# Two decode attentions on one core: the output layouts of step 31 moved ahead of A's wo matmuls, and the result's transposition in bf16

## The chip, the cores and the metric

The kernel runs on one core of a Trainium2 chip. The metric is the time of one execution on the device in microseconds. The kernel before took 675.33 us, the median of 3 runs from 673.68 to 675.58 us.

A core has five engines with a queue of instructions each: PE (TensorE, matrix products), DVE (VectorE), ACT (ScalarE), POOL (GpSimd) and SP (SyncE, which here issues the transfers). An engine works through its own queue in order and waits for others by semaphores.

## What is computed

Two attention blocks, A and B, decode one token each, with the same sizes: 32 heads of 128 elements, a cache of 8192 positions per head, a model width of 512. Everything is bf16. For each block:

```python
q = (x @ wq).reshape(B, Sq, H, Dh).transpose(0, 2, 1, 3)   # B = Sq = 1, H = 32, Dh = 128
scores = einsum("bhqd,bhkd->bhqk", q, k_cache) * Dh ** -0.5
p = softmax(scores, axis=-1)
o = einsum("bhqk,bhkd->bhqd", p, v_cache)
y = o.transpose(0, 2, 1, 3).reshape(B, Sq, H * Dh) @ wo     # wo is 4096 x 512
```

The output is y of A and y of B side by side, 1024 numbers. The caches of the two blocks are 256 MB and each byte of them is used once.

## The kernel before

**Steps.** A step handles one pair of heads: n = 0 to 15 are A's pairs, 16 to 31 are B's. Each pair has 4 MB of keys and 4 MB of values. A tile kn or vn holds one pair: the first head's positions lie on partitions 0 to 63, the second's on 64 to 127, 128 positions on each partition. There are two buffers of each.

**The scores.** DVE multiplies kn in place by the query, in four instructions of 32 positions each (`plan_mul`, L292). PE sums over the 128 elements of a head in two halves of 16 matmuls with the identity, accumulating in PSUM down to 8 columns per position (`plan_red`, L301), and DVE reduces the 8 (`plan_sr`, L310). These 32 matmuls of a step are called a batch here. Then come the maximum (`plan_max` L316 on DVE, `plan_gmax` L322 on PE and L325 on DVE, `plan_exp` L335 on PE and L339 on ACT), the exponentials on ACT (L346) and their sum (`plan_sum`: L351 on PE, the reciprocal L354 on DVE).

**The values.** `plan_pv` (L367) runs 128 matmuls with vn as weights and two columns of probabilities each. They belong to the pair before the one whose scores are being worked on, and lie between that step's score instructions. `plan_o` (L377) scales the result into oD, which holds for each head the 128 outputs on 128 partitions.

**The output product.** wo arrives in SBUF with 32 rows of wo on each partition for A, and for B in five groups of heads (0 to 15, 16 to 23, 24 to 27, 28 and 29, 30 and 31), which `WOG` lists. A group of h heads has h rows on each partition. The columns of oD have to be laid out to match: `plan_relayout` multiplies them with a mask into zb on DVE (L402), sums with a selection matrix on PE (L406, into the PSUM tile misc) and copies the result to o2 on DVE (L408). zb has two buffers and misc has one, so each matmul L406 waits for the copy L408 before it. `plan_wo` (L419) then multiplies wo with o2: four matmuls of one column for each head, all accumulating in the PSUM tile qyp; 128 in all for A. `plan_y` (L426) copies qyp to yT, 128 partitions by 4 columns for each block. At the end `plan_out` transposes yT with one matrix product against an identity (L430), DVE rounds the result to bf16 (L433), and SP writes 2 KB out.

**The order of the work.** There is no planner: a loop over n from 0 to 32 appends instructions to the queues of the five engines, and the order of the calls is the order in each queue. Ahead of an instruction stand the waits for what it needs. Between steps 3 and 30, PE's queue is emitted as a loop over two steps; step 31 and what follows is straight code. All large transfers are issued by SP. In step n these are the keys of step n + 1 and the values of step n, each waiting until its buffer is free. In step 31 SP issues the last values in two halves and then the five groups of B's wo, which go to the buffer of A's wo and so wait for A's last wo matmul (`load_wo`: `wo_done[0]`).

**Around the change.** At the start of step 31 (`L1` is 31) the kernel brings in the output product of A and B's first three groups, whose pairs are done by then. Later in step 31, behind the first two multiplications, DVE copies A's result (`plan_y(0)`). B's fourth and fifth group are laid out at the ends of steps 31 and 32, and B's 128 wo matmuls come last.

```python
if n == L1:
    plan_relayout(0, 0)
    plan_wo(0, 0)
    for g in range(3):
        plan_relayout(1, g)
```

Of the kernel before, what the change touches and what calls it, by code (L numbers as in the profile page):

```python
# [8 lines left out]
BF16 = mybir.dt.bfloat16  # L9
F32 = mybir.dt.float32  # L10

P = 128
# [11 lines left out]
class _Plan:  # L24
# [6 lines left out]
    def wait(self, eng, mark):  # L31
        if mark is None:
            return
        ctr, val = mark
        if val <= 0 or self.waited.get((eng, ctr.name), 0) >= val:
            return
        self.waited[(eng, ctr.name)] = val
        self.prog[eng].append((None, ctr, val))

    def op(self, eng, fn, ctr=None, needs=(), inc=1):  # L40

        for m in needs:
            self.wait(eng, m)
        self.prog[eng].append((fn, ctr, inc))
        if ctr is None:
            return None
        ctr.n += inc
        return ctr, ctr.n
# [46 lines left out]
def bass_concat_heads__mha_block_cached__gqa_block_cached__decode_kernel(  # L95
# [18 lines left out]
    NA = 2  # L114
# [22 lines left out]
    with ExitStack() as st:  # L137
# [3 lines left out]
        def sb(name, shape, dt):  # L141
            return ec(nc.sbuf_tensor(name, shape, dt))
# [14 lines left out]
        ident = sb("ident", [P, P], BF16)  # L157
        ident_f = sb("ident_f", [P, P], F32)
# [9 lines left out]
        mask = {g: sb("mask%d" % g, [P, P // g], BF16) for g in RG}  # L168
        jsel = {g: sb("jsel%d" % g, [P, g], BF16) for g in RG}
        NQ = NOUT // P  # L170
        yT = sb("yT", [P, NA, NQ], F32)
        out_q = sb("out_q", [NA * NQ, P], BF16)

        def ps(name, shape):
# [25 lines left out]
        def dma(eng, dst, src, c, needs=()):  # L200
            return op(eng, lambda e: e.dma_start(dst, src), c, needs, inc=16)  # L201
# [24 lines left out]
        def load_k(n):  # L226
            a, i = divmod(n, PA)
            src = ks[a][0, 2 * i:2 * i + 2].rearrange("h (p t) d -> (h p) (t d)", p=HP)
            k_in[n] = dma("SP", kn[:, n % NK].rearrange("p t d -> p (t d)"), src, s_k[n % NK],
                          [red_done.get(n - NK)])  # L230

        def load_v(n, parts=1):
            a, i = divmod(n, PA)
            src = vs[a][0, 2 * i:2 * i + 2].rearrange("h (p t) d -> (h p) (t d)", p=HP)
            dst = vn[:, n % NV].rearrange("p t d -> p (t d)")
            w = T * Dh // parts
            v_in[n] = [dma("SP", dst[:, i * w:(i + 1) * w], src[:, i * w:(i + 1) * w],
                           s_v2 if i else s_v[n % NV],
                           [q_done[1] if n == 1 else pv_done.get(n - NV)])
                       for i in range(parts)]  # L240
# [4 lines left out]
        def load_wo(a, g):  # L245
            h0, n = WOG[a][g]
            src = wos[a][h0 * Dh:(h0 + n) * Dh, :].rearrange("(p j) n -> p (j n)", p=P)
            wo_in[a, g] = dma("SP", wo_sb[:, h0:h0 + n, :].rearrange("p j n -> p (j n)"), src, s_wo[g],
                              [q_done[0] if a == 0 else wo_done[0]])
# [16 lines left out]
        def plan_q(a, j):  # L266

            def mm(e):
                r = None
                for hh in range(2):  # L270
                    for c in range(C):
                        w = wq_sb[a][:, c, 8 * j * Dh:8 * (j + 1) * Dh].rearrange(
                            "p (i h d) -> p i h d", h=2, d=Dh)[:, :, hh, :]
                        r = e.matmul(  # L274
                            qyp[hh * HP:(hh + 1) * HP, :].rearrange("p (i d) -> p i d", d=Dh),
                            xb[:, a, c, hh * HP:(hh + 1) * HP], w,
                            start=(c == 0), stop=(c == C - 1))
                return r
            m = op("PE", mm, c_pe, [x_ready, wq_in[a], qy_free[0]])
            q_done[a] = m  # L280
            n0 = a * PA + 4 * j
            qy_free[0] = op("ACT", lambda e: e.copy(
                qbc[:, n0:n0 + 4, :].rearrange("p i d -> p (i d)"), qyp[:]), c_act, [m])
            for n in range(n0, n0 + 4):
                qbc_ready[n] = qy_free[0]
# [4 lines left out]
        def plan_mul(n, c):  # L290
            k = kn[:, n % NK, c * CT:(c + 1) * CT, :]
            mul_done[n, c] = op("DVE", lambda e: e.tensor_tensor(  # L292
                k, k, qbc[:, n:n + 1, :].broadcast_to([P, CT, Dh]), ALU.mult),
                c_mul, [k_in[n], qbc_ready[n]])
# [101 lines left out]
        def plan_relayout(a, g):  # L396
            h0, n = WOG[a][g]
            z = z_n[0] % 2
            z_n[0] += 1
            s = P // n  # L400
            zv = zb[:, z, :].rearrange("p (h s) -> p h s", s=s)
            m = op("DVE", lambda e: e.tensor_tensor(  # L402
                zv, oD[:, a, h0:h0 + n].unsqueeze(2).broadcast_to([P, n, s]),
                mask[n][:, None, :].broadcast_to([P, n, s]), ALU.mult),
                c_dve, [sel_ready[n], o_done[a * PA + (h0 + n) // 2 - 1], z_free.get(z)])
            z_free[z] = op("PE", lambda e: e.matmul(misc[:, 0:n], zb[:, z, :], jsel[n][:],  # L406
                                                    start=True, stop=True), c_pe, [m, misc_free[0]])
            o2_ready[a, g] = misc_free[0] = op("DVE", lambda e: e.tensor_copy(  # L408
                o2[:, a, h0:h0 + n], misc[:, 0:n]), c_dve, [z_free[z]])

        def plan_wo(a, g):

            h0, n = WOG[a][g]

            def mm(e):
                r = None
                for j in range(h0, h0 + n):
                    for i in range(NQ):
                        r = e.matmul(qyp[:, i:i + 1], wo_sb[:, j, i * P:(i + 1) * P],  # L419
                                     o2[:, a, j:j + 1], start=(j == 0 and i == 0),  # L420
                                     stop=(j == H - 1 and i == NQ - 1), skip_group_check=True)
                return r
            wo_done[a] = op("PE", mm, c_pe, [o2_ready[a, g], wo_in[a, g], qy_free[0]])

        def plan_y(a):
            qy_free[0] = op("DVE", lambda e: e.tensor_copy(yT[:, a, :], qyp[:, 0:NQ]), c_dve,  # L426
                            [wo_done[a]])

        def plan_out():
            m = op("PE", lambda e: e.matmul(bmp[0:NA * NQ, 0:P], yT[:].rearrange("p a q -> p (a q)"),  # L430
                                            ident_f[:], start=True, stop=True),
                   c_pe, [qy_free[0], nb_done[NP - 1]])
            m = op("DVE", lambda e: e.tensor_copy(out_q[:], bmp[0:NA * NQ, 0:P]), c_dve, [m])  # L433
            done = dma("SP", out[0].rearrange("o (q n) -> (o q) n", q=NA * NQ), out_q[:], s_out, [m])
            wait("SP", done)
# [11 lines left out]
        for n in range(NP + 1):  # L447
            marks[n] = len(pl.prog["PE"])
            last = n == NP
            if n == L1:  # L450
                plan_relayout(0, 0)
                plan_wo(0, 0)
                for g in range(3):
                    plan_relayout(1, g)
            if n + 1 < NP:
                load_k(n + 1)
            if n == 1:
                for j in range(4):
                    plan_q(1, j)
            if not last:  # L460
                load_v(n, 2 if n == NP - 1 else 1)
            if n == 12:
                load_wo(0, 0)
            if n == NP - 1:
                for g in range(len(WOG[1])):
                    load_wo(1, g)
            if not last:
                plan_mul(n, 0)
                plan_mul(n, 1)
            if n == L1:  # L470
                plan_y(0)
            if n > 0:
                plan_sum(n - 1)
            if not last:
                plan_red(n, 0)
                plan_mul(n, 2)
                plan_mul(n, 3)
                plan_sr(n, 0)
                plan_red(n, 1)
            if n > 0:  # L480
                plan_pv(n - 1, 0, HT)
            if not last:
                plan_sr(n, 1)
                plan_max(n)
                plan_gmax(n)
            if n > 0:
                plan_pv(n - 1, HT, T)
            if not last:
                plan_exp(n)
            if n > 0:  # L490
                plan_o(n - 1)
            if n >= L1:
                plan_relayout(1, n - L1 + 3)
        for g in range(len(WOG[1])):
            plan_wo(1, g)
        plan_y(1)
        plan_out()

        for name, at in (("SP", block.sync), ("PE", block.tensor), ("ACT", block.scalar),
# [38 lines left out]
```

## Time and profile before

| | before |
|---|---|
| median of the runs | 675.33 us (673.68 to 675.58) |
| the profiled execution | 675.39 us |
| its span, first to last instruction | 673.7 us |
| mean granted clock of PE | 0.744 |
| PE busy | 469.2 us (70%) |
| DVE busy | 359.5 us (53%) |
| ACT busy | 43.9 us (7%) |
| read from HBM | 285.21 MB, 423 GB/s over the span |

All times inside the execution are microseconds from the start of the span. The profile's page gives the busy time of the engines, the span in 40 slices with the granted clock and the share in which the transfer engines were busy, the chain of work that ended last, and groups of equal instructions. The trace behind it gives the same chain in order of time, the timeline of each engine, and for each transfer the time from issue to landing. In a timeline a row has its start, its duration, the engine and line, the output and the input with their shapes, and how many instructions are merged in it; square brackets hold the idle time of the engine just before it and what ended that.

Matmuls of PE are pipelined: a row of 128 matmuls with 164 ns each lasts 3.6 us, not 21.

### The profile page before, as it was taken

Reading aid. Unit: us, or ns where it says so; the run is one execution under the profiler, and the core shown is the slowest. Engines: PE = TensorE matmul, PEld = TensorE weight load, DVE = VectorE, ACT = ScalarE, POOL = GpSimd, SP = SyncE. Lnnn points to the kernel's source line nnn. Section 1 sums busy time; section 2 is a strip of 40 time slices with the busy share of each in tenths; the row PEclk is TensorE's granted clock in tenths of the full one; section 3 lists DMA queues with packets and bytes.
Section 4 is the critical chain, followed back from the end, with each engine's and each line's share of the span. In section 5 each row is a group of like instructions: output and inputs, shape, how many; then the busy total and the mean of one; then the engine's idle time right before and its main releaser. Section 6 shows DMA issues by size and latency. Waiting matters only on the chain.

```text
span 673.7 us, 12421 instructions
## 1 busy us (share of the span) xinstructions
PE 469.2 (70%) x5712; PEld 275.7 (41%) x5712; DVE 359.5 (53%) x345; ACT 43.9 (7%) x171; POOL 2.1 (0%) x13
## 2 busy tenths in 40 slices
PE   2665887667678766665677787766768875666977
PEld 1223444344444433442344444434444442344637
DVE  1553556566555665615655555656555565655361
ACT  1120000000000000000000000000000000000000
POOL 1000000000000000000000000000000000000000
PEclk9997877666787766776667887766788776678765
DMA  9999999999999999999999999999999999999994
GB/s 374 436 435 431 435 427 426 427 432 436 432 432 434 428 434 426 434 434 434 430 430 432 430 430 434 434 434 432 426 436 428 432 434 432 430 434 427 432 423 182
DMA packets 10547, 285.43 MB, mean 424 GB/s; under 512 B 1186, under 2 KB 1188, under 8 KB 1572
## 3 DMA queue, kind: packets, MB, share of 16 engines
q1 hardware_dynamic: 10528, 285.22, 98.6%
q8 instruction: 10, 0.16, 0.1%
q14 instruction: 5, 0.04, 0.0%
q10 hardware_dynamic: 4, 0.00, 0.0%
HBM read 285.21 MB, written 0.00 MB: 423 GB/s over the span
## 4 chain that ended last, share of the span: by engine, by line
DMA 61%; PE 26%; DVE 8%; issue 4%; ACT 0%; SPq 0%; ACTq 0%
DMA kn<-in_A_k_cache_dram 31%; DMA kn<-in_B_k_cache_dram 30%; PE rps L301 23%; DVE kn L292 7%; PE acc L367 1%; PE qyp L419 1%; PE bmp L335 0%; ACT pt L346 0%; PE misc L406 0%; DVE zb L402 0%; DVE o L408 0%; PE mtp L322 0%; PE bmp L430 0%; PE misc L351 0%; SPq L201 0%
## 5 line engine op out<-in xcount | busy, mean ns | idle before, releaser
L301 PE MATMUL rps<-kn,ident 128*128 128x512 bf16 x1024 | 292.3, 456 | 143.3 <-DVE kn L292 143.3
L292 DVE TENSOR_TENSOR kn<-kn,qbc 128x4096 bf16<-128x4096 bf16 x128 | 286.8, 2284 | 92.1 <-DMA kn<-in_A_k_cache_dram 62.1
L301 PEld LDWEIGHTS rps<-kn,ident 128*128 128x128 bf16 x1024 | 113.6, 114 | 309.7 <-DVE kn L292 141.9
L367 PEld LDWEIGHTS acc<-pt,vn 128*128 128x128 bf16 x4096 | 110.6, 97 | 14.3 <-issue 6.9
L310 DVE TENSOR_REDUCE s_sb<-rps 128x64 f32<-128x512 f32 x64 | 44.3, 692 | 131.2 <-PE rps L301 131.2
L367 PE MATMUL acc<-pt,vn 128*128 128x2 bf16 x4096 | 112.9, 164 | 0.0
L351 PE MATMUL misc<-rsum,ones_f 128*128 128x2 f32 x64 | 18.2, 354 | 39.2 <-ACT pt L346 38.8
L339 ACT ACTIVATE negb<-bmp 128x1 f32<-128x1 f32 x32 | 5.5, 171 | 594.5 <-PE bmp L335 594.5
L351 PEld LDWEIGHTS misc<-rsum,ones_f 128*128 128x128 f32 x64 | 15.5, 300 | 42.2 <-ACT pt L346 41.4
L377 DVE TENSOR_TENSOR oD<-acc,rinv 128x2 bf16<-128x2 f32 x32 | 5.1, 160 | 47.7 <-PE acc L367 47.7
L346 ACT ACTIVATE pt<-s_sb,negb 64x128 bf16<-64x128 f32 x64 | 27.9, 435 | 1.8
L335 PE MATMUL bmp<-gm,hrow 1*128 1x1 f32 x128 | 23.9, 287 | 0.5 <-DVE gm L325 0.5
L325 DVE TENSOR_REDUCE gm<-mtp 1x2 f32<-1x128 f32 x32 | 8.9, 279 | 27.8 <-PE mtp L322 27.8
L335 PEld LDWEIGHTS bmp<-gm,hrow 1*128 1x128 f32 x128 | 21.2, 233 | 1.3 <-issue 0.7
L322 PE MATMUL mtp<-ident_f,m 128*1 128x128 f32 x64 | 12.1, 271 | 1.1 <-DVE m L316 1.1
L274 PE MATMUL qyp<-wbuf,xb 128*64 128x512 bf16 x32 | 7.7, 633 | 6.3 <-DMA wbuf<-in_A_wq_dram 4.3
L346 ACT ACTIVATION_READ_ACCUMULATOR pt<-s_sb,negb 64x1 f32 x64 | 11.7, 182 | 0.0
L316 DVE TENSOR_REDUCE m<-s_sb 128x1 f32<-128x128 f32 x32 | 9.2, 287 | 1.1
L419 PE MATMUL qyp<-o,wbuf 128*128 128x1 bf16 x256 | 7.1, 165 | 0.3 <-DVE o L408 0.3
L419 PEld LDWEIGHTS qyp<-o,wbuf 128*128 128x128 bf16 x256 | 7.0, 104 | 0.4 <-DVE o L408 0.4
L274 PEld LDWEIGHTS qyp<-wbuf,xb 128*64 128x64 bf16 x32 | 2.4, 158 | 11.0 <-issue 6.3
L354 DVE RECIPROCAL rinv<-misc 128x2 f32<-128x2 f32 x32 | 5.3, 165 | 1.6 <-PE misc L351 1.6
(34 smaller groups left out, 29.1 us busy)
## 6 DMA issues: line engine op xcount, KB each, us to landing
kn<-in_A_k_cache_dram SPq DMA_DIRECT2D x16, 4096.0 KB, 25.5
vn<-in_A_v_cache_dram SPq DMA_DIRECT2D x16, 4096.0 KB, 31.5
kn<-in_B_k_cache_dram SPq DMA_DIRECT2D x16, 4096.0 KB, 25.2
vn<-in_B_v_cache_dram SPq DMA_DIRECT2D x15, 4096.0 KB, 31.4
wbuf<-in_A_wq_dram SPq DMA_DIRECT2D x1, 4096.0 KB, 12.2
vn<-in_B_wq_dram SPq DMA_DIRECT2D x1, 4096.0 KB, 30.7
wbuf<-in_A_wo_dram SPq DMA_DIRECT2D x1, 4096.0 KB, 40.8
vn<-in_B_v_cache_dram SPq DMA_DIRECT2D x2, 2048.0 KB, 18.1
```

The lines of the kernel that those rows point to most:

```text
L274: r = e.matmul(qyp[hh * HP:(hh + 1) * HP, :].rearrange("p (i d) -> p i d", d=Dh), xb[:, a, c, hh * HP:(hh + 1) * HP], w, start=(c == 0), s ...
L292: mul_done[n, c] = op("DVE", lambda e: e.tensor_tensor(k, k, qbc[:, n:n + 1, :].broadcast_to([P, CT, Dh]), ALU.mult), c_mul, [k_in[n], qbc ...
L301: r = e.matmul(rps[:, h, :].rearrange("p (t d) -> p t d", d=DW), ident[:], kn[:, n % NK, h * HT:(h + 1) * HT, i * DW:(i + 1) * DW], start= ...
L310: sr_done[n, h] = op("DVE", lambda e: e.tensor_reduce(s_sb[:, n % 2, h * HT:(h + 1) * HT], rps[:, h, :].rearrange("p (t d) -> p t d", d=DW ...
L316: m_done[n] = op("DVE", lambda e: e.tensor_reduce(m1[:, n % 2:n % 2 + 1], s_sb[:, n % 2, :], AX.X, ALU.max), c_dve, [sr_done[n, 1]])
L322: m = op("PE", lambda e: e.matmul(mtp[0:1, 0:P], m1[:, n % 2:n % 2 + 1], ident_f[:], start=True, stop=True), c_pe, [m_done[n], i_identf, g ...
L325: gm_done[n] = op("DVE", lambda e: e.tensor_reduce(gm[:, n % 2, :], mtp[0:1, 0:P].rearrange("o (h p) -> o h p", h=2), AX.X, ALU.max), c_dv ...
L335: r = e.matmul(bmp[:, 0:1], hrow[0:1, h, :], gm[0:1, n % 2, h:h + 1], start=(h == 0), stop=(h == 1))
L346: p_done[n] = op("ACT", lambda e, h=h, q=q: e.activation(pt[q, n % 2, :, h], s_sb[q, n % 2, :], AF.Exp, bias=negb[q, n:n + 1], scale=scale ...
L351: m = op("PE", lambda e: e.matmul(misc[:, 0:2], ones_f[:], rsum[:, n % 2, :], start=True, stop=True), c_pe, [p_done[n], misc_free[0]])
L367: r = e.matmul(acc[:, n % 2, 0:2], vn[:, n % NV, t, :], pt[:, n % 2, t, :], start=(t == 0), stop=(t == T - 1))
L419: r = e.matmul(qyp[:, i:i + 1], wo_sb[:, j, i * P:(i + 1) * P], o2[:, a, j:j + 1], start=(j == 0 and i == 0), stop=(j == H - 1 and i == NQ ...
```

## The change

In step 31 the calls are reordered: the layouts of B's first three groups come ahead of A's wo matmuls, so that the four layouts of outputs (one of A, three of B) stand together in front. Only PE's queue changes by this, since `plan_wo` issues nothing on another engine. SP's loads of B's wo wait for the same matmuls as before.

The tile yT becomes bf16 instead of fp32, so `plan_y` rounds each block's result when it leaves PSUM, and the transposition at the end is a bf16 product with the bf16 identity.

```diff
-        yT = sb("yT", [P, NA, NQ], F32)
+        yT = sb("yT", [P, NA, NQ], BF16)
...
         def plan_out():
             m = op("PE", lambda e: e.matmul(bmp[0:NA * NQ, 0:P], yT[:].rearrange("p a q -> p (a q)"),
-                                            ident_f[:], start=True, stop=True),
+                                            ident[:], start=True, stop=True),
                    c_pe, [qy_free[0], nb_done[NP - 1]])
...
             if n == L1:
                 plan_relayout(0, 0)
-                plan_wo(0, 0)
                 for g in range(3):
                     plan_relayout(1, g)
+                plan_wo(0, 0)
```

## The prediction

> **What bounds the kernel now.** First the page: the engines' shares, the slices and the chain that ended last.
>
> ```profile
> PEclk9997877666787766776667887766788776678765
> DMA  9999999999999999999999999999999999999994
> DMA 61%; PE 26%; DVE 8%; issue 4%; ACT 0%; SPq 0%; ACTq 0%
> ```
>
> The transfers run without a gap until the last slice, so nothing before about step 30 can be won on an engine: DVE waits there for each kn (1.62 us at 618.04, in the waits of step 30). The last kn stands differently. Its load, issued at 612.66, took 24.8 us by its issue row, so it landed at 637.46; the multiplications that read it begin at 642.61. From 618.04 on the chain holds only engines. Here it is in order of time around step 31:
>
> ```profile
> 637.58 3.57 PE qyp L419 x128
> 641.15 0.05 PE misc L406
> ...
> 641.23 0.17 DVE o L408
> ...
> 642.69 0.78 DVE kn L292
> ...
> 647.15 9.66 PE rps L301 x32
> ```
>
> It goes through A's 128 wo matmuls (L419), one relayout matmul (L406) and DVE's copy (L408) to the multiplications (L292) and the reduction (L301). The timeline of DVE shows the stall. Columns: start, us, instruction, count, idle before and its releaser.
>
> ```profile
> 637.44 0.28 DVE L402 TENSOR_TENSOR zb<-oD,mask 128x128 bf16<-128x128 bf16 x1
> 641.23 0.17 DVE L408 CAST o<-misc 128x16 bf16<-128x16 f32 x1 [3.50 <-PE misc L406]
> 641.32 0.28 DVE L402 TENSOR_TENSOR zb<-oD,mask 128x128 bf16<-128x128 bf16 x1
> 641.88 0.17 DVE L408 CAST o<-misc 128x8 bf16<-128x8 f32 x1 [0.28 <-PE misc L406]
> ...
> 642.61 4.48 DVE L292 TENSOR_TENSOR kn<-kn,qbc 128x4096 bf16<-128x4096 bf16 x2
> 647.01 0.16 DVE L426 COPY yT<-qyp 128x4 f32<-128x4 f32 x1
> ```
>
> DVE has zb for B's first group ready at 637.72, but its matmul stands behind 128 others on PE, so DVE idles 3.50 us with the last kn already in SBUF.
>
> **The order, step by step.** PE gets the three matmuls of B's groups before A's 128; no instruction is added. From the rows at 641.32 and 641.66 a zb is followed by its matmul after 0.34 us and by its copy 0.22 us later, and the next zb comes 0.09 us on. With zb at 637.44 the matmul starts at 637.78, the copy at 638.00 instead of 641.23. All that follows on DVE moves by **3.23 us**: the multiplications start at 642.61 - 3.23 = 639.38, still 1.92 us after the kn landed.
>
> A's 128 matmuls now start after the third B matmul, at 642.30 - 3.23 + 0.1 = 639.2, and take 3.57 us (row at 637.58): done at 642.8. The sum of step 30 (L351, 0.6 us) follows to 643.4. The reduction needs the second multiplication, at 647.15 - 3.23 = 643.92. So the 3.57 us are hidden under two multiplications (4.48 us), with 0.5 us to spare on PE. DVE's copy yT (L426) stands behind those multiplications, at 643.8; it waits for the 128 matmuls, with 1.0 us to spare. Behind it are the reciprocal and the third multiplication; without the cover each us of lateness would reach the second half of the reduction.
>
> On SP, the five loads of B's wo wait for A's matmuls: from 641.18 to about 642.8, 1.6 us later. Only the output's DMA is queued behind them. The 4.2 MB of the last vn stand before them on the transfer engines until 656.9 (its second half: issued 636.57, 20.3 us), so I cost the delay at nothing; without that cover it would be up to 1.6 us on each landing. ACT and POOL issue nothing that moves; ACT's exponentials of step 30 end at 638.4.
>
> **The clock.** The 32 matmuls of a step's reduction do not always take the same time:
>
> ```profile
> 564.29 8.44 PE L301 MATMUL rps<-kn,ident 128*128 128x512 bf16 x32 [6.00 <-DVE kn L292]
> 583.73 8.96 PE L301 MATMUL rps<-kn,ident 128*128 128x512 bf16 x32 [5.00 <-DVE kn L292]
> 603.16 9.47 PE L301 MATMUL rps<-kn,ident 128*128 128x512 bf16 x32 [4.47 <-DVE kn L292]
> 622.59 9.99 PE L301 MATMUL rps<-kn,ident 128*128 128x512 bf16 x32 [4.15 <-DVE kn L292]
> 647.15 9.66 PE L301 MATMUL rps<-kn,ident 128*128 128x512 bf16 x32 [3.75 <-DVE kn L292]
> ```
>
> In short windows the granted clock is 0.50 at the start of a batch and 1.00 later. The mean is 0.79 in 652 to 653, so it rises at 652.42; by the same reading it falls at 659.24 and had risen at about 628.5. These distances, 6.82 and 23.9, are 2 and 7 times 3.41: the changes come on a grid of 3.41 us. Batch 31 waited 5.27 us for its rise, batch 30 5.93: 0.66 us of waiting cost 9.99 - 9.66 = 0.33, half of it. Starting at 643.92, batch 31 would rise at 652.42 - 3.41 = 649.01, after 5.09 us, and take 9.66 - 0.09 = 9.57. **Gain 0.09 us.** The 3.57 us of A's matmuls now stand close before the batch. I give them no influence on the clock: from 662.7 to 670.9 PE is almost filled with matmuls of one or two columns and the clock stays 0.50.
>
> [...]
>
> **The end.** With yT in bf16 the last transposition is one matmul, not two passes:
>
> ```profile
> 671.13 0.60 PE L430 MATMUL bmp<-ident_f,yT 128*8 128x128 f32 x2 [0.25 <-DVE yT L426]
> 671.76 0.28 DVE L433 CAST out_q<-bmp 8x128 bf16<-8x128 f32 x1 [0.69 <-PE bmp L430]
> ```
>
> From matmul to copy it is 0.63 us. A bf16 matmul of 16 columns is followed by its copy after 0.22 us (641.01 to 641.23); 112 columns more, at 0.43 us per 512 (the batches' spacing at clock 0.50), add 0.09: 0.31. That is **0.3 us** less, on the path. Bounds: 0 (one pass as dear as two) and 0.41 (as the 16 columns); I take 0.3, the row of its own type. DVE's copies to yT (158 ns) write half the bytes; I leave them at that price.
>
> **Sum.** The profiled execution took 675.39 us, 1.72 more than its span, which I leave alone. 675.39 - 3.23 - 0.09 - 0.30 = 671.77; it stands 0.06 above the median of the runs, so **671.7 us**.
>
> **What is late next.** All else on the chain moves with DVE: the last value product from 663.15 to 659.8 (its vn landed at 656.9), B's wo matmuls from 667.33 to 664.0. Their loads landed at 661.9, 664.4, 665.5, 666.2 and 666.8 by the issue rows; at 27.3 ns per matmul (3.49/128) they are wanted at 664.0, 665.8, 666.6, 667.1 and 667.3. So only 0.5 us is left before the last load becomes the bound. From 666.8 the end can follow no sooner than the last eight matmuls and the tail allow: yT's copy at about 667.16 instead of 670.91, 3.75 us, and 0.3 for the transposition, 671.3 us. This floor matters because a rise of the clock can come 2.7 to 6.1 us after a batch starts, depending on where the grid lies; two batches carry the chain. With the grid 3.2 us earlier, batch 30 would rise after 2.7 us and take 8.4, batch 31 start 1.6 us sooner, rise after 3.6 and take 8.85: 2.4 us less than profiled for before (its fastest run was 673.68), while after would stop at 671.3 there and in most positions. Forecast's own range: 671.3 to 672.1 (no gain at the end).
>
> **Rivals.** (1) The chain moves, but B's wo loads are late. If their landing moves with their issue, 1.6 us, the last comes at 668.4 and the floor is 671.3 + 1.6 = 672.9 us. Against it: DMA share about 1.0 from 640 to 658. For it: the share falls to 0.72 and 0.60 at 663 and 664, where the small loads go.
>
> (2) The last kn takes DVE's place as the bound. It has 1.92 us; if it landed at 641.2, half the gain would be left: about 673.5. For it: all earlier steps wait for kn. Against: the loads in front of it are issued as before.
>
> (3) Slower: A's 128 weight loads now run beside DVE's multiplications of the same SBUF, as they do nowhere in before; there DVE idled. PE would hold the batch if the 128 took longer. They end at 639.2 + 128c, with 0.6 for the sum; the whole gain of 3.6 us is gone when that reaches 647.4, c = 59 ns instead of 27.3. If nothing overlapped any more but the weight loads' own time (104 ns a row), it would be 653.1, 5.7 us later than that, about 681. Against: the reductions keep 0.43 us per matmul with DVE multiplying, and a multiplication takes 2.28 us either way; but they load weights sixteen times less often. Lower bound 0.
>
> [...]
>
> (4) The change doesn't do what it says at the end: the transposition costs the same. That is the forecast's upper end, 672.1.
>
> **Chances.** Forecast with (4) 0.78; rival 1 0.12; rival 2 0.05; rival 3 0.05. What a measurement of this kernel can tell from no change is about 0.3%, 2.0 us. The forecast is 0.54% below the median and counts as faster; rival 1 (0.36%) I split in half, since before may lie lower on another grid; rival 2 is within; rival 3 slower. Faster 0.84, same 0.11, slower 0.05. The range holds the forecast and rival 1, with 0.4 us for the loads' own pace on both sides: 670.9 to 673.2.
>
> **What would show it.** Right: DVE's stall of 3.50 us gone, multiplications at about 639.4 with no wait for kn; the 128 L419 matmuls beside them in 3.6 us; L430 as x1 and about 0.3 us to its copy. Wrong: a wait for kn at L292 (rival 2), B's wo matmuls waiting for wbuf by more than a few tenths (rival 1), L419 above 59 ns each (rival 3). A batch 31 much below 9.5 us from a different position on the grid would lie below my sum but not below the floor.

## The result and the profile after

| | before | after |
|---|---|---|
| median of the runs | 675.46 us (673.68 to 675.77, 4 runs) | 671.73 us (671.58 to 671.83, 4 runs) |
| the profiled execution | 675.39 us | 671.83 us |
| its span | 673.7 us | 670.0 us |
| mean granted clock of PE | 0.744 | 0.751 |

The ratio is 0.995, with a 95% interval from 0.9933 to 0.9967: the changed kernel is faster by about 0.5%. Its time is the one predicted, 671.7 us. Note the spread: the runs of before lie up to 2.1 us apart, those of after 0.25. That was the first hint that something else ends the kernel now.

The page after, the same three lines as shown of before (granted clock, transfers' share, chain by engine), and the queue that carries instructions:

```profile
PEclk9997786667887766685778877666887666787876
DMA  9999999999999999999999999999999999999996
...
q8 instruction: 10, 0.16, 0.1%
...
DMA 65%; PE 23%; DVE 8%; issue 4%; SPq 0%
```

The share of transfers in the chain has grown from 61% to 65% and that of PE has fallen from 26% to 23%. The timeline of DVE at the start of step 31:

```profile
635.74 0.28 DVE L402 TENSOR_TENSOR zb<-oD,mask 128x128 bf16<-128x128 bf16 x1
636.30 0.17 DVE L408 CAST o<-misc 128x16 bf16<-128x16 f32 x1 [0.28 <-PE misc L406]
...
637.68 4.48 DVE L292 TENSOR_TENSOR kn<-kn,qbc 128x4096 bf16<-128x4096 bf16 x2
642.08 0.15 DVE L426 CAST yT<-qyp 128x4 bf16<-128x4 f32 x1
```

The stall of 3.50 us in front of the copy L408 of B's first group has become 0.28 us. From B's first zb to the multiplications it is 637.68 - 635.74 = 1.94 us, against 642.61 - 637.44 = 5.17 before: 3.23 us less. L426 follows the multiplications without idle time, so A's product was ready. PE shows why:

```profile
637.42 3.55 PE L419 MATMUL qyp<-o,wbuf 128*128 128x1 bf16 x128
640.84 0.57 PE L351 MATMUL misc<-rsum,ones_f 128*128 128x2 f32 x2
642.22 9.20 PE L301 MATMUL rps<-kn,ident 128*128 128x512 bf16 x32 [0.82 <-DVE kn L292]
```

A's 128 matmuls take 3.55 us beside the multiplications, as they took 3.57 alone, and PE then waits 0.82 us for DVE, not DVE for PE. The end of the same timeline:

```profile
661.89 0.40 PE L419 MATMUL qyp<-o,wbuf 128*128 128x1 bf16 x9 [0.29 <-DMA wbuf<-in_B_wo_dram]
662.72 1.60 PE L419 MATMUL qyp<-o,wbuf 128*128 128x1 bf16 x55 [0.43 <-issue]
664.61 1.02 PE L419 MATMUL qyp<-o,wbuf 128*128 128x1 bf16 x32 [0.28 <-DMA wbuf<-in_B_wo_dram]
665.82 1.02 PE L419 MATMUL qyp<-o,wbuf 128*128 128x1 bf16 x24 [0.19 <-DMA wbuf<-in_B_wo_dram]
667.19 0.35 PE L419 MATMUL qyp<-o,wbuf 128*128 128x1 bf16 x8 [0.35 <-DMA wbuf<-in_B_wo_dram]
667.79 0.27 PE L430 MATMUL bmp<-ident,yT 128*8 128x128 bf16 x1 [0.25 <-DVE yT L426]
```

B's 128 wo matmuls, one uninterrupted row of 3.55 us at 667.33 before, now start 5.4 us earlier and fall into pieces: each group waits for its load. Of the 5.4 us the order gives 3.2. Two batches were shorter in this execution (more on which below), which gives 1.7, and the matmuls of L335 behind each of them took 0.60 us instead of 1.0, which gives 0.8; 0.3 us go to the wait for the first load. The chain of waits ends accordingly (start, us, what):

```profile
643.81 23.24 DMA wbuf<-in_B_wo_dram
667.05 0.14 issue
667.19 0.37 PE qyp L419 x8
...
667.58 0.17 DVE yT L426
...
667.79 0.28 PE bmp L430
```

The last load of B's wo lands at 667.05 and only eight matmuls and the tail follow. The bound has moved from the engines to the transfers.

### The profile page after: what moved, and what is told of

It reads as the page before. It is cut to its first block, busy times and chain, and to the rows that moved or that the text cites. A ratio compares the mean times of both kernels' runs of the same rounds, so it can differ in the third digit from the quotient of the medians.

```text
span 670.0 us, 12418 instructions
## 1 busy us (share of the span) xinstructions
PE 470.0 (70%) x5711; PEld 274.8 (41%) x5711; DVE 359.4 (54%) x345; ACT 43.9 (7%) x171; POOL 2.1 (0%) x13
## 4 chain that ended last, share of the span: by engine, by line
DMA 65%; PE 23%; DVE 8%; issue 4%; SPq 0%
DMA kn<-in_A_k_cache_dram 31%; DMA kn<-in_B_k_cache_dram 30%; PE rps L301 22%; DVE kn L292 7%; DMA wbuf<-in_B_wo_dram 3%; PE qyp L419 1%; PE acc L367 0%; SPq L201 0%; PE misc L406 0%; DVE zb L402 0%; DVE o L408 0%; PE bmp L335 0%; PE mtp L322 0%; PE bmp L430 0%; DVE out_q L433 0%
## 5 line engine op out<-in xcount | busy, mean ns | idle before, releaser
L335 PE MATMUL bmp<-gm,hrow 1*128 1x1 f32 x128 | 22.8, 278 | 0.5 <-DVE gm L325 0.5
L335 PEld LDWEIGHTS bmp<-gm,hrow 1*128 1x128 f32 x128 | 20.2, 222 | 1.3 <-issue 0.7
L419 PE MATMUL qyp<-o,wbuf 128*128 128x1 bf16 x256 | 7.9, 165 | 1.6 <-DMA wbuf<-in_B_wo_dram 1.1
L419 PEld LDWEIGHTS qyp<-o,wbuf 128*128 128x128 bf16 x256 | 7.4, 104 | 2.1 <-DMA wbuf<-in_B_wo_dram 1.0
```

The lines of the kernel that those rows point to most:

```text
L335: r = e.matmul(bmp[:, 0:1], hrow[0:1, h, :], gm[0:1, n % 2, h:h + 1], start=(h == 0), stop=(h == 1))
```

## Experiments

In what follows, "the changed kernel" is the one of the prediction. The pieces of the chain were taken apart first, then the new bound was moved.

**The new order alone.** yT and the identity go back to fp32.

```diff
-        yT = sb("yT", [P, NA, NQ], BF16)
+        yT = sb("yT", [P, NA, NQ], F32)
...
-                                            ident[:], start=True, stop=True),
+                                            ident_f[:], start=True, stop=True),
```

> The new order alone: yT and the transposition stay in fp32. My theory: the new order frees the chain on the engines, and the last load of B's wo becomes the bound; the transposition comes after that bound and adds its full difference, 0.3 us (matmul to copy 0.63 us instead of 0.31). Expected 671.73 + 0.3 = 672.0 us, last load landing at about 667.0, and runs within about 0.3 us of each other. Rival, the transposition is off the path: 671.7 us. Rival, most of the gain is the rounding's: above 674 us.

Measured: 672.29 us (672.03 to 673.68, 10 runs), ratio 0.9962 [0.9953, 0.9972]. The transposition and DVE's last two instructions in its profile:

```profile
667.57 0.16 DVE L426 COPY yT<-qyp 128x4 f32<-128x4 f32 x1 [5.05 <-PE qyp L419]
667.78 0.59 PE L430 MATMUL bmp<-ident_f,yT 128*8 128x128 f32 x2 [0.26 <-DVE yT L426]
668.42 0.28 DVE L433 CAST out_q<-bmp 8x128 bf16<-8x128 f32 x1 [0.69 <-PE bmp L430]
```

L426 stands at 667.57, as in the changed kernel (667.58), but from L430 to L433 it is 0.64 us, not 668.10 - 667.79 = 0.31. The order carries nearly all of the gain; the transposition adds 0.33 us by its rows, behind the last load (the medians lie 0.56 us apart). One run at 673.68 is wider than expected, and why is not known.

**The bf16 transposition alone.** The diff of the change without its last part; `plan_wo(0, 0)` stays in front of the three layouts.

> The bf16 transposition alone, the old order. My theory: DVE's stall of 3.5 us behind A's wo matmuls stays, the multiplications of step 31 follow it, and only the 0.3 us at the end go: 0.3 below the kernel before, about 675.2 us where the batches of 32 matmuls last as in its profile, and down to about 672.7 where the clock rises earlier. The runs of the kernel before differ by 2.1 us, so the rows decide: matmul to copy 0.31 us instead of 0.63, and 3.5 us of idle time on DVE in front of L408. Rival, the rounding carries the gain: 671.7 us.

Measured: 674.62 us (673.11 to 675.67, 10 runs), ratio 0.9995 [0.9983, 1.0007]: the time can't show 0.3 us here. The rows do:

```profile
641.07 0.17 DVE L408 CAST o<-misc 128x16 bf16<-128x16 f32 x1 [3.50 <-PE misc L406]
...
671.24 0.27 PE L430 MATMUL bmp<-ident,yT 128*8 128x128 bf16 x1 [0.25 <-DVE yT L426]
671.55 0.28 DVE L433 CAST out_q<-bmp 8x128 bf16<-8x128 f32 x1 [0.36 <-PE bmp L430]
```

The stall of 3.50 us is unchanged, and the transposition takes 0.31 us. The rounding does not carry the gain.

**B's wo loads issued 10 us later.** This is rival 1 of the prediction.

```diff
                 plan_red(n, 1)
+            if n == NP - 1:
+                wait("SP", red_done[n])
+                for g in range(len(WOG[1])):
+                    load_wo(1, g)
```

The same loop further up is taken out.

> As the changed kernel, but SP holds B's five wo loads back until batch 31 has ended (about 651 us instead of 641). My theory: the last vn occupies the transfer engines until about 657, so the loads only queue behind it; they land when the bytes ahead of them are through, the last at about 667.0 as before, and the time stays at 671.7 us within 0.3. Rival (rival 1 of the prediction): a landing moves with its issue; the last one then comes at about 677 and the time is 681 to 682 us.

Measured: 672.05 us (671.76 to 672.15, 5 runs), ratio 0.9958 [0.9942, 0.9973]. In its profile SP issues the five loads at 651.62 instead of 641.00, the last load lands at 667.08 instead of 667.05, and the last eight matmuls start at 667.21 instead of 667.19. Rival 1 falls: a landing here depends on the bytes in front of it, not on its issue. The median is 0.3 us above that of the changed kernel; the profiled execution (671.76 us) shows nothing of this.

**Half of B's wo not loaded.** Groups 2 to 5 use what A's wo left in those rows, and wait for the first group alone.

```diff
             if n == NP - 1:
-                for g in range(len(WOG[1])):
-                    load_wo(1, g)
+                load_wo(1, 0)
+                for g in range(1, len(WOG[1])):
+                    wo_in[1, g] = wo_in[1, 0]
```

> As the changed kernel, but of B's five wo loads only the first (2 MB) is made; B's product leaves out the other 2 MB of wo and uses what A left in those rows, with the same instructions. My theory: the last load is then no bound, B's 128 wo matmuls run without a wait, and the engines' chain ends it again: 669.5 us where the clock rises as in the changed kernel's profile (yT's copy at 665.2 instead of 667.6), and anything from 669.3 to 671.8 by the position of the clock's grid, so the runs differ by more than the 0.25 us of the changed kernel's. Rival, the chain and not the loads ends the changed kernel: 671.7 us, as close together as before.

Measured: 670.39 us (670.06 to 671.27, 6 runs), ratio 0.9935 [0.992, 0.995]. The direction is as expected: 1.3 us less, and a wider spread, so the loads did bound the changed kernel. But it is 0.9 us above the expected 669.5. PE's timeline shows something I had left out:

```profile
661.78 0.40 PE L419 MATMUL qyp<-o,wbuf 128*128 128x1 bf16 x9
662.66 3.31 PE L419 MATMUL qyp<-o,wbuf 128*128 128x1 bf16 x119 [0.49 <-issue]
```

There is no wait for a load behind the first matmul, but a pause after the ninth in which PE waits for nothing the profile shows. The changed kernel has it too (0.43 us at 662.72), the new order alone 1.24 us.

**One more megabyte.** A load of 1 MB into a buffer that nobody reads any more, queued ahead of B's wo, in the changed kernel and in the kernel before.

```diff
             if n == NP - 1:
+                extra = dma("SP", kn[:, 0, 0:CT].rearrange("p t d -> p (t d)"),
+                            ks[0][0, 0:2].rearrange("h (p t) d -> (h p) (t d)", p=HP)[:, 0:CT * Dh],
+                            s_k[0], [red_done[NP - 2]])
                 for g in range(len(WOG[1])):
...
+            wait("SP", extra)
             done = dma("SP", out[0].rearrange("o (q n) -> (o q) n", q=NA * NQ), out_q[:], s_out, [m])
```

> The changed kernel with one more load of 1 MB (from a key cache into the buffer of step 30's kn, which nobody reads any more), queued in front of B's wo loads. My theory: the changed kernel ends by its transfers, so every byte in front of the last landing counts: 1.05 MB at 434 GB/s are 2.4 us, 671.7 + 2.4 = 674.1 us. Rival, the engines' chain still ends it and has room: 671.7 us.

Measured: 674.64 us (674.52 to 674.87, 10 runs). The last eight matmuls start at 669.59 instead of 667.19, which is 2.40 us for the 2.4 expected. Most of the rest of the 2.9 us came after the output's transfer was issued: from there to the end of the span it is 1.97 us, and 1.60 in before and in the changed kernel. These 0.37 us stand in all four profiles with the extra load (1.97 or 1.98 us) and are not explained. The runs stay within 0.35 us. The changed kernel ends by its transfers.

> The kernel before with the same extra load of 1 MB. My theory: its engines' chain ends 3.75 us after its transfers would let it, so 2.4 us more of transfers are hidden: 675.4 us where the batches last as in its profile, with single runs not below about 674. Rival, the transfers end this kernel too: 677.9 us.

Measured: 675.65 us (674.82 to 677.21, 10 runs) against 674.45 for the kernel before on the same chip, ratio 1.0018 [1.0005, 1.0031]. Five of ten runs lie at 674.8 to 675.3, about where they were expected, but not for the reason given. The end of B's wo matmuls in the profile, an execution of 675.25 us:

```profile
666.47 3.12 PE L419 MATMUL qyp<-o,wbuf 128*128 128x1 bf16 x111 [1.30 <-issue]
669.84 0.35 PE L419 MATMUL qyp<-o,wbuf 128*128 128x1 bf16 x8 [0.25 <-DMA wbuf<-in_B_wo_dram]
```

The last eight matmuls wait for their load, so this execution ends by its transfers too: the megabyte was not hidden, it has used up the room that the kernel before had. An estimate of that floor is the changed kernel's 671.73 us, plus 2.40 for the bytes, 0.37 behind the output's transfer and 0.33 for the transposition in fp32: 674.83, and the lowest run is 674.82. Above it, three of ten runs lie at 677.0 to 677.2, above any run of before. So something of 1 to 2 us was missing in my account, in both kernels.

**The pause after the ninth matmul.** PE's code outside its loop is loaded during the run: the page counts ten instruction loads of 16 KB on queue q8, and in the trace of the changed kernel none of them starts from 121 to 642 us, in which the loop runs. One of them starts at 660.4 and takes 1.1 us; PE goes on at 662.72. In no profile of before, after or the kernels above does PE pass the ninth matmul sooner than 2.3 us after such a load starts. Sixty-four matmuls in front of all others move the code by half of such a piece (128 pairs of weight load and matmul, as a count below shows). First with half of B's wo not loaded:

```diff
+        def pad(e):
+            for _ in range(63):
+                e.matmul(misc[:, 0:1], ones_bf[:], ones_bf[:, 0:1], start=True, stop=True)
+            return e.matmul(misc[:, 0:1], ones_bf[:], ones_bf[:, 0:1], start=True, stop=True)
+        op("PE", pad, c_pe, [i_onesb])
+
         for a in range(NA):
             def xmm(e, a=a):
```

> The kernel with half of B's wo loads left out, plus 64 matmuls of one column at the very start of PE's queue (their result is overwritten). In every profile that shows a pause of 'issue' in B's wo matmuls it stands after the ninth, and a 16 KB load of instructions ends 1.4 us before PE goes on. Theory: PE's straight code comes in pieces of 16 KB (128 pairs of weight load and matmul) through the same transfer engines, and the ninth matmul is the end of a piece. Then 64 pairs more in front move the end of the piece 64 pairs earlier in the work: the pause after the ninth wo matmul is gone and, if there is one, it stands in the last value product after its 74th matmul. The pause only changes place: 670.4 us within 0.5. Rival, the pause belongs to the wo matmuls or their data: it stays after the ninth.

Measured: 670.12 us (669.95 to 670.85, 4 runs). The lines of this kernel are numbered six higher (L425 is L419):

```profile
657.58 3.62 PE L373 MATMUL acc<-pt,vn 128*128 128x2 bf16 x128
...
662.22 3.57 PE L425 MATMUL qyp<-o,wbuf 128*128 128x1 bf16 x128 [0.26 <-DMA wbuf<-in_B_wo_dram]
```

The pause is gone; the value product is 0.07 us longer, and the first load is what is late now. Then the same 64 matmuls in the kernel before with 1 MB more, beside that kernel again:

> The kernel before with the extra load of 1 MB, plus 64 matmuls of one column at the start of PE's queue. The kernel with the extra load alone ran from 674.8 to 677.2 us, three of its ten runs at 677.0 to 677.2, above every run of the kernel before (at most 675.9). Theory: those are runs whose batches are long, so that the engines' chain comes as late as in the profile of before, with the pause for instructions after the ninth of B's wo matmuls (1.3 us in its profile) on top; the code moved by half a piece takes the pause out of the wo matmuls, and no run lies above 676.0 us. Rival, the extra load itself delays the chain in those runs: some runs at 677 us again, with no pause after the ninth matmul.

> The kernel before with the extra load of 1 MB again, unaltered, on the chip of the run beside it. Both theories: runs between 674.8 and 677.3 us, some of them above 676.5, with the pause after the ninth of B's wo matmuls in its profile.

Measured: 676.40 us (675.12 to 676.67, 10 runs) with the 64 matmuls, 675.09 us (674.88 to 676.93, 10 runs) without. The second kernel's profile fell on its slowest run:

```profile
667.06 0.38 PE L419 MATMUL qyp<-o,wbuf 128*128 128x1 bf16 x9
668.55 3.34 PE L419 MATMUL qyp<-o,wbuf 128*128 128x1 bf16 x119 [1.11 <-issue]
```

Here the chain comes as late as in the profile of before (667.33) and the pause and the 0.37 us behind the output's transfer stand on top: that is the run at 676.93. The three runs at 677.0 to 677.2 were not profiled; that they are of this kind is likely, not shown. The runs above 676.5 are one of ten here and three of ten in the run before it. With the 64 matmuls the next boundary of the code comes into the wo matmuls, and the pause with it:

```profile
666.80 2.08 PE L425 MATMUL qyp<-o,wbuf 128*128 128x1 bf16 x73
669.76 1.61 PE L425 MATMUL qyp<-o,wbuf 128*128 128x1 bf16 x55 [0.88 <-issue]
```

73 is 9 + 64. I had expected no run above 676.0 and no pause, having forgotten that next boundary; seven of ten runs lie above. The pause is thus shown to belong to a place in the code and not to the data. The rival (no pause, still slow) is not what this profile shows either. Why the median with the 64 matmuls is 1.3 us higher is open.

**More instruction loads, and the changed kernel once more.** 256 such matmuls in front, two whole pieces, and beside it the changed kernel unaltered.

> The changed kernel plus 256 matmuls of one column (32 KB of instructions) at the very start of PE's queue, before the first keys have landed. Theory: each 16 KB load of instructions holds up one of the 16 transfer engines by about 1.1 us, the engines stay apart from then on, and the last landing waits for the latest one. Two more such loads: 12 instead of 10, and the last landing 0 to 1.4 us later, by which engine they fall on; time 671.7 to 673.2 us. The pause after the ninth wo matmul stays where it is, since the code moves by two whole pieces. Rival, the loads of instructions cost the transfers nothing: 671.7 us and the same distance between the first and the last engine.

> The changed kernel again, unaltered, on the chip of the two runs beside it. By my theory it ends by its last load: 671.7 us, runs within about 0.3 us, while the kernel before spreads over 2 us.

Measured: 671.87 us (671.59 to 672.60, 4 runs) and 671.85 us (671.81 to 671.98, 4 runs). Two loads more cost nothing that can be measured; the pause stays near its place, after ten wo matmuls.

## Why the prediction held, step by step

- **The order, 3.23 us.** Right, and to the hundredth in the rows (5.17 to 1.94 us). No cover failed: A's matmuls lie beside the multiplications, yT's copy has no idle time, and the late issue of B's loads does not move their landing (667.08 against 667.05), even with ten more microseconds.
- **The last kn.** Right in this execution, but with far less room than the 1.92 us counted: it landed at 637.43 and the multiplications start at 637.68, since batch 30 was shorter. In the second profile of the changed kernel, batch 30 took 8.36 us; kn landed at 637.28, the multiplications start at 637.30, and PE waits 1.01 us for them instead of 0.82. So rival 2 begins there, with 0.2 us, which the loads of wo hide.
- **The clock.** The rule that a batch is longer by half of what it waits for the rise was right, the position not mine to choose. In the profile after, batch 30 took 8.78 us instead of 9.99 and batch 31 9.20 instead of the 9.57 I had written. The mean clock in 646 to 647 is 0.73, so it rises at 646.54, 4.32 us after the batch starts; the rule of half a microsecond each gives 9.66 - (5.27 - 4.32)/2 = 9.19. That A's matmuls do not raise the clock held as well: they run from 637.42 to 640.97, and the granted clock is 0.50 in every microsecond from 637 to 646. In each of the two traces all changes of the clock from 31 us on lie whole multiples of 3.41 us apart. The grid lies differently in the two executions: the rise in batch 31 comes at 652.42 us in the one and at 646.54 in the other, 5.88 us or 1.72 of these 3.41 apart, and the two batches of the chain take 19.65 us and 17.98.
- **The transposition, 0.3 us.** Right: 0.31 instead of 0.63.
- **The sum, 671.77.** Right as a number, but it is the sum of a chain that does not end the measured kernel, so the agreement to 0.1 us is luck. What ends it is the floor by B's loads, which the prediction had as "what is late next" at 671.3. It did say that the kernel would stop there in most positions of the grid, but the number it gave as the forecast was that of the other chain. In the profiled execution (671.83) the floor came out 0.5 higher: the last load landed at 667.05 instead of 666.8, the last eight matmuls with their wait took 0.17 us more than I counted, and 0.1 us lie outside the span. The kernels with half of B's wo give 670.1 and 670.4 us, so without the later loads the changed kernel would take 1.3 to 1.6 us less, and its engines' chain ended that much earlier than the sum. Most of this is shorter batches: 8.97 and 9.29 us in the profile of the second of these kernels, against 9.99 and 9.57 in the sum.
- **What was missing: the pause for instructions.** It did no harm to the forecast, because in the profiles of the changed kernel PE waits for a later load behind the pause, or for the first load in front of it (1.41 us in the second profile, where no pause is seen).
- **Rivals.** Rival 1 fell with the late loads; B's wo matmuls do wait for wbuf, by 0.19 to 0.35 us before each of four groups, which is not more than the few tenths the prediction allowed. Rival 3, slower by weight loads beside DVE: 3.55 us for 128 beside the multiplications and 3.57 without them, so nothing to be seen, and the multiplications keep 4.48 us for two. Rival 2 shows only as the 0.2 us above.

## What to carry to other kernels

On an in-order engine, put the short work that another engine waits for ahead of the long work that nobody waits for yet: here one matmul behind 128 cost DVE 3.5 us. Before you count the whole stall as gain, work out which wait is late next and at what time it would end the kernel; here 3.7 us could be won, and anything more would have been lost to transfers that run without a gap from the start (busy 90% or more in 39 of the 40 slices). When the runs of the changed kernel suddenly lie close together, suspect that the bound is now one that does not vary.

## What the runs showed of the hardware

The pause for instructions was not expected. PE consumes a pair of weight load and matmul in 27.3 ns in these rows. With 256 pairs more the loads of instructions were 12 instead of 10, so a piece holds 128 pairs and lasts 3.5 us. In every profile PE passes the boundary 2.3 us after the load starts or later; what differs is how late the load starts. In the kernel before it starts 1.93 us after the last value product does, with the transfers' share at 0.33 in the microsecond around that moment, and PE does not pause. The same kernel with 1 MB more has a share of 0.81 and 1.04 there in its two profiles; the load starts 3.10 and 3.36 us after the value product, and PE pauses 1.11 and 1.30 us. So the pause seems to grow when the load has to come through transfer engines that are full. It does not vanish whenever they are nearly empty: the bf16 transposition alone (share 0.23, load after 2.37 us) pauses 0.3 us, and half of B's wo (0.11, after 2.65 us) 0.49 us.

The 16 transfer engines do not finish together. By the arrival marks in the trace, they deliver a load within 0.4 to 0.6 us of each other at 42 us, and within 3.1 to 3.6 us at the last load; with two more instruction loads by then, two engines are already 1.7 us behind the others at 43 us, and with one more (the kernels with 64 matmuls in front) it is one engine, 1.8 to 1.9 us behind. So an engine seems to fall back by an instruction load and not to catch up. That the kernel's last landing could be earlier with less code was not tried, and two loads more did not make it later, so the link to the end stays open.
